# Loading q and k eight rows at a time in a channel-attention and GLU kernel

## The chip, the cores and the metric

One core of a Trainium2 chip. The metric is the device time of one execution in microseconds (us). Repeated executions of one kernel mostly agree within 0.3 us. The page of a profile is one profiled execution; its span is some 2 us shorter than the time. A line of a timeline gives start in us, duration in us, engine, line, operation, output<-inputs.

## The reference, cut to what matters

```python
# q, k, v: (4, 6016, 256) float32; tau = 1
qn = q / (norm(q, axis=1) + 1e-6)            # norms over the 6016 rows
kn = k / (norm(k, axis=1) + 1e-6)
a = softmax(kn.transpose(0, 2, 1) @ qn / tau)  # 256 x 256 per batch
x = (v @ a).reshape(24064, 256)
gate = sigmoid(x @ w_gate); val = x @ w_val    # 256 -> 1536
out = (gate * val) @ w_out                     # 1536 -> 256
```

## The kernel before

The rows of a batch lie 47 to a partition (6016 / 128). q, k and v are read from HBM as float32 and cast to bf16 by the DMA, four rows at a time: twelve groups a batch (in batch 0 thirteen, as the last group is split in two and one). For each group, PE adds eight matmuls of 256 columns to the scores s = q^T k, and VectorE (DVE) and ScalarE (ACT) square q and k for the norms.

Batch 0 is the head of the program: nothing can run beside it, since the weights of the later work, G = a^T w_gate / row sums and H likewise, need the whole batch. Batches 1 to 3 have their scores mixed into the GLU work of the batch before, at fixed places ("slots": one slot is one of the twelve 128-column parts of the hidden layer for one chunk of 512 rows). In the head, "fillers" keep PE working between groups: matmuls whose result nobody reads.

```python
def load_qk(b, t0, nt):                          # groups of four rows
    tiles = []
    for name, src in (("q", q), ("k", k)):
        tl = qkpool.tile([P, TPC, C], BF16, tag=name, name=name + "_sb")
        nc.gpsimd.dma_start(out=tl[:, :nt, :], in_=rows(src, b)[:, t0 : t0 + nt, :])
        tiles.append(tl)
    qk[b, t0] = tiles
...
for g, (t0, nt) in enumerate(groups0):           # the head
    engines = (nc.vector, nc.scalar) if g < last0 else (nc.scalar, nc.vector)
    sq = [squares(0, t0, nt, w, engines[w], acc[w] if g == 0 else None) for w in range(2)]
    if 0 < g < n_acc:                            # n_acc is 9
        for w in range(2):
            nc.vector.tensor_tensor(out=acc[w], in0=acc[w], in1=sq[w], op=ALU.add)
    for u in range(nt):
        score(0, t0, u)                          # 2 matmuls a row
    if g < n_acc:
        busy(5)                                  # five fillers
    elif g == n_acc:
        norm_mms(ps_n0, acc, TPC, True, False)
        norm_mms(ps_n0, sq, nt, False, False)
    elif nt == TPC:
        busy(2)
        norm_mms(ps_n0, sq, nt, False, False)
    ...                                          # groups 11 and 12
norms_sqrt(0); ...; norms_inv(0); ...            # 1 / norms, on ACT and DVE
spread_k(0, 0, pso, "o"); ...                    # ps_rk: needs 1 / norms
...
load_v(0, 1)                                     # POOL's DMAs, in this order
nc.gpsimd.dma_start(out=w_out_sb, in_=moe_w_out.rearrange("(t p) c -> p t c", p=P))
```

v is transposed by DMA (issued by SP), one transpose a chunk; only the first two chunks of batch 0 are transposed by PE.

Of the kernel before, what the change touches and what calls it, by code (L numbers as in the profile page):

```python
# [10 lines left out]
BF16 = mybir.dt.bfloat16  # L11
# [6 lines left out]
def kernel(  # L18
# [21 lines left out]
    P = nc.NUM_PARTITIONS  # L40
# [4 lines left out]
    B, N, C = q.shape  # L45
    CW, DFF = moe_w_gate.shape
    assert CW == C and C % P == 0 and N % P == 0 and DFF % P == 0
    NT = N // P
# [4 lines left out]
    TPC = 4  # L53
    CH = TPC * P
    NCH = (NT + TPC - 1) // TPC
    groups = [(t, min(TPC, NT - t)) for t in range(0, NT, TPC)]

    head = NT - NT % TPC
    groups0 = groups[: head // TPC] + [(t, n) for t, n in ((head, NT % TPC - 1), (NT - 1, 1)) if n > 0]

    def rows(x, b):
        return x[b].rearrange("(p t) c -> p t c", p=P)
# [3 lines left out]
    def pool(name, bufs, **kw):  # L66
        return ctx.enter_context(tc.tile_pool(name=name, bufs=bufs, **kw))

    consts = pool("consts", 1)
    qkpool = pool("qkpool", NCH)  # L70
    sqpool = pool("sqpool", 2)
    attp = pool("attp", 1)
    ghpool = pool("ghpool", 2)
# [13 lines left out]
    def mm(out, lhsT, rhs, start, stop, **kw):  # L87
        nc.tensor.matmul(out, lhsT=lhsT, rhs=rhs, start=start, stop=stop, **kw)  # L88


    qk = {}

    def load_qk(b, t0, nt):
        tiles = []
        for name, src in (("q", q), ("k", k)):
            tl = qkpool.tile([P, TPC, C], BF16, tag=name, name=name + "_sb")
            nc.gpsimd.dma_start(out=tl[:, :nt, :], in_=rows(src, b)[:, t0 : t0 + nt, :])  # L97
            tiles.append(tl)
        qk[b, t0] = tiles

    vs = {}

# [5 lines left out]


    t0, nt = groups0[0]  # L110
    qk[0, 0] = [qkpool.tile([P, TPC, C], BF16, tag=n, name=n + "_sb") for n in ("q", "k")]
    first_f32 = [consts.tile([P, nt, C], FP32, name=f"first{w}") for w in range(2)]
    for eng, tl, src in zip((nc.sync, nc.scalar), first_f32, (q, k)):
        eng.dma_start(out=tl, in_=rows(src, 0)[:, t0 : t0 + nt, :])
    nc.scalar.preload_act_table(ACT.Sqrt)
    load_qk(0, *groups0[1])

    ident_bf = consts.tile([P, P], BF16)
    make_identity(nc, ident_bf)
# [8 lines left out]

    nc.vector.tensor_copy(out=qk[0, 0][0], in_=first_f32[0])
    nc.scalar.copy(qk[0, 0][1], first_f32[1])  # L130
    for t0, nt in groups0[2:]:
        load_qk(0, t0, nt)
    load_v(0, 0)

# [18 lines left out]
    def score(b, t0, u):  # L153
        q_sb, k_sb = qk[b, t0]
        if t0 == 0 and u == 0:
            st.setdefault(b, {})["s"] = pss.tile([P, CB, C], FP32, tag="s", name="ps_s")
        ps_s = st[b]["s"]
        t = t0 + u
        for j in range(CB):
            mm(  # L160
                ps_s[:, j, :],
                q_sb[:, u, ds(j * P, P)],
                k_sb[:, u, :],
                start=(t == 0 and j == 0),
                stop=(t == NT - 1),
                skip_group_check=True,
            )

    def squares(b, t0, nt, which, engine, sq=None):
        src = qk[b, t0][which]  # L170
        if sq is None:
            sq = sqpool.tile([P, TPC, C], BF16, tag=f"sq{which}", name=f"sq{which}")
        if engine is nc.scalar:
            nc.scalar.activation(out=sq[:, :nt, :], in_=src[:, :nt, :], func=ACT.Square)  # L174
        else:
            engine.tensor_tensor(  # L176
                out=sq[:, :nt, :], in0=src[:, :nt, :], in1=src[:, :nt, :], op=ALU.mult
            )
        return sq

    def norm_mms(ps, sqs, nt, first, last, order=(0, 1)):

        for w in order:
            sq = sqs[w]
            for u in range(nt):
                for j in range(CB):
                    mm(
                        ps[:, w * CB + j : w * CB + j + 1],
                        sq[:, u, ds(j * P, P)],
                        ones_bf[:, 0:1],  # L190
                        start=(first and w == order[0] and u == 0 and j == 0),
                        stop=(last and u == nt - 1),
                        skip_group_check=True,
                    )
# [171 lines left out]
    def transpose_v(b, ci, ps=None, late=None):  # L366

        t0, nt = groups[ci]
        v_sb = vs.pop((b, ci))
        vT = vtpool.tile([P, TPC * CB, P], BF16, tag="vT", name="vT")  # L370
        flat = v_sb[:, :nt, :].rearrange("p t c -> p (t c)")
        if ps is None:
            nc.sync.dma_start_transpose(out=vT[:, : nt * CB, :], in_=flat)
        else:
            for n in range(nt * CB):
                nc.tensor.transpose(  # L376
                    out=ps[:, n, :], in_=flat[:, ds(n * P, P)], identity=ident_bf
                )
            half = nt * CB // 2
            nc.vector.tensor_copy(out=vT[:, :half, :], in_=ps[:, :half, :])  # L380
            (nc.scalar.copy if late is None else late)(vT[:, half : nt * CB, :], ps[:, half : nt * CB, :])
        vts[b, ci] = vT.rearrange("p (u cb) n -> p cb u n", cb=CB)
# [54 lines left out]
    def busy(n):  # L437

        ps = psg.tile([P, CH], FP32, tag="g", name="ps_busy")
        for _ in range(n):  # L440
            mm(ps, ones_bf, ones_wide, True, True)
# [8 lines left out]
    for g, (t0, nt) in enumerate(groups0):  # L450
        engines = (nc.vector, nc.scalar) if g < last0 else (nc.scalar, nc.vector)
        sq = [squares(0, t0, nt, w, engines[w], acc[w] if g == 0 else None) for w in range(2)]
        if 0 < g < n_acc:
            for w in range(2):
                nc.vector.tensor_tensor(out=acc[w], in0=acc[w], in1=sq[w], op=ALU.add)  # L455
        for u in range(nt):
            score(0, t0, u)
        if g < n_acc:
            busy(5)
        elif g == n_acc:  # L460
            norm_mms(ps_n0, acc, TPC, True, False)
            norm_mms(ps_n0, sq, nt, False, False)
# [3 lines that stand above are left out]
        elif g < last0:  # L466
            held = (sq, nt)
        else:
            norm_mms(ps_n0, *held, False, False)
            norm_mms(ps_n0, sq, nt, False, True, (1, 0))  # L470
# [28 lines left out]
    def side_work(b):  # L499


        side = {}

        def at(slot, fn, *a):
            side.setdefault(divmod(slot, FC), []).append((fn, a))

        for ci in range(NCH):
            nb, nci = (b, ci + 1) if ci + 1 < NCH else (b + 1, 0)
            lb, lci = (b, ci + 2) if ci + 2 < NCH else (b + 1, ci + 2 - NCH)
            if (nb, nci) == (0, 1):  # L510
                at(7, lambda: transpose_v(0, 1, psm.tile([P, TPC * CB, P], BF16, tag="m", name="ps_tp")))
            elif nb < B:
                at(ci * FC + 2, transpose_v, nb, nci)
            if lb < B:
                at(ci * FC + 0, load_v, lb, lci)
        n = b + 1
        if n == B:
            return side
        first, last = (14 if b == 0 else 0), 9 * FC
        for g, (t0, nt) in enumerate(groups):  # L520
            s0 = first + g * (last - first) // NCH
            at(max(0, s0 - 20), load_qk, n, t0, nt)
            for u in range(nt):
                at(first + (t0 + u) * (last - first) // NT, score, n, t0, u)
            if g == 0:
                at(s0, acc_start, n)
            for i, (fn, w) in enumerate(((acc_square, 0), (acc_add, 0), (acc_square, 1), (acc_add, 1))):
                at(s0 + 1 + 2 * i, fn, n, g, w)
        at(9 * FC + 9, norms_mm, n)
        for ci, s, *call in (  # L530
            (9, 0, wide_sqrt, n),
            (9, 2, wide_inv, n, 0),
            (9, 3, wide_inv, n, 1),
            (10, 0, wide_scale, n),
            (10, 0, exps, n, 0),
            (10, 0, exps, n, 1),
        ):
            side.setdefault((ci, FC + s), []).append((call[0], call[1:]))
        at(11 * FC + 0, sums_both, n)
        at(11 * FC + 0, gh_tiles, n)  # L540
        for i in range(len(gh_order)):
            at(11 * FC + min(i + 1, FC - 1), gh, n, i, *((pss, "s"), (psm, "m"))[i % 2])
        return side
# [61 lines left out]
```

## Time and profile before

| | before |
|---|---|
| time, median of 6 | 831.43 us (831.34 to 831.52) |
| PE busy | 817.8 of 829.6 us |
| granted PE clock | full, one core |
| packets on the loads' queue q0 | 23,920 |
| head: scores of group 10 begin | 31.73 us |
| head: norm matmuls end, ps_rk begins | 34.39, 35.30 us |

The prediction shows the lines on PE's waits, its timeline in the head and the traffic of the DMA queues. Three more matter later. They are from the timelines of PE, DVE and POOL (start in us, duration in us, engine, line, operation, output<-inputs), all of the kernel before, at the end of the head:

```profile
35.30 0.68 PE L88 MATMUL ps_rk<-ident_f,r 128*128 128x128 f32 x4
```

```profile
34.77 0.17 DVE L265 TENSOR_SCALAR r<-r 128x4 f32<-128x4 f32 x1
34.98 0.18 DVE L266 RECIPROCAL r<-r 128x4 f32<-128x4 f32 x1
```

### The profile page before, as it was taken

Reading aid. Unit: us, or ns where it says so; the run is one execution under the profiler, and the core shown is the slowest. Engines: PE = TensorE matmul, PEld = TensorE weight load, DVE = VectorE, ACT = ScalarE, POOL = GpSimd, SP = SyncE. Lnnn points to the kernel's source line nnn. Section 1 sums busy time; section 2 is a strip of 40 time slices with the busy share of each in tenths; the row PEclk is TensorE's granted clock in tenths of the full one; section 3 lists DMA queues with packets and bytes.
Section 4 is the critical chain, followed back from the end, with each engine's and each line's share of the span. In section 5 each row is a group of like instructions: output and inputs, shape, how many; then the busy total and the mean of one; then the engine's idle time right before and its main releaser. Section 6 shows DMA issues by size and latency. Waiting matters only on the chain.

```text
span 829.6 us, 13793 instructions
## 1 busy us (share of the span) xinstructions
PE 817.8 (99%) x5224; PEld 503.6 (61%) x5224; DVE 581.1 (70%) x998; ACT 391.9 (47%) x644; POOL 83.3 (10%) x159
## 2 busy tenths in 40 slices
PE   7899999999999999999999999999999999999998
PEld 4556666666666666665576666666566566666666
DVE  6577777777667777777767777777766666666664
ACT  4654444445644444444654444444655444444442
POOL 5531100002110100000210020000000000000000
PEclk9999999999999999999999999999999999999999
DMA  9999724326755553233874453233222323322211
GB/s 209 207 206 185 134 52 90 51 62 131 135 107 102 102 108 62 51 52 84 156 140 100 84 113 73 51 78 63 61 61 64 71 51 83 70 49 69 46 36 71
DMA packets 78739, 77.19 MB, mean 93 GB/s; under 512 B 50768, under 2 KB 55632, under 8 KB 78672
## 3 DMA queue, kind: packets, MB, share of 16 engines
q0 software_dynamic: 23920, 38.81, 28.3%
q1 hardware_dynamic: 54608, 36.97, 17.4%
q8 instruction: 41, 0.67, 0.3%
q10 hardware_dynamic: 144, 0.52, 0.2%
q14 instruction: 26, 0.21, 0.1%
HBM read 78.64 MB, written 24.64 MB: 125 GB/s over the span
## 4 chain that ended last, share of the span: by engine, by line
PE 95%; DMA 3%; POOL 0%; issue 0%; ACT 0%; DVE 0%; POOLq 0%; ACTq 0%
PE ps_o L88 30%; PE ps_val L88 29%; PE ps_gate L88 29%; PE ps_s L88 4%; DMA k_sb<-in_k_dram 3%; PE ps_gh L88 3%; PE ps_n L88 0%; PE ps_busy L88 0%; POOL q_sb L97 0%; ACT e_sb L294 0%; DVE hT L406 0%; ACT g_sb L405 0%; POOL k_sb L97 0%; PE ps_rk L88 0%; PE ps_tp L376 0%
## 5 line engine op out<-in xcount | busy, mean ns | idle before, releaser
L406 DVE TENSOR_TENSOR hT<-ps_val,g_sb 128x512 bf16<-128x512 f32 (+1 forms) x576 | 391.5, 680 | 214.6 <-ACT g_sb L405 209.3
L405 ACT ACTIVATE g_sb<-ps_gate 128x512 bf16<-128x512 f32 (+1 forms) x576 | 338.5, 589 | 386.0 <-PE ps_gate L88 378.4
L88 PE MATMUL ps_gate<-vT,gh_G 128*128 128x512 bf16 (+1 forms) x1152 | 337.7, 375 | 0.4 <-ACT g_sb L405 0.4
L88 PE MATMUL ps_val<-vT,gh_H 128*128 128x512 bf16 (+1 forms) x1152 | 337.5, 375 | 0.1
L88 PE MATMUL ps_o<-w_out_sb,hT 128*128 128x256 bf16 x2256 | 326.2, 273 | 0.0
L88 PEld LDWEIGHTS <-hT 128*128 128x128 bf16 x2256 | 220.8, 98 | 124.7
L88 PEld LDWEIGHTS <-gh_H 128*128 128x128 bf16 x1152 | 112.7, 98 | 131.0 <-issue 0.4
L88 PEld LDWEIGHTS <-gh_G 128*128 128x128 bf16 x1152 | 112.4, 98 | 38.0 <-issue 0.6
L106 POOL DMA_DIRECT2D v_sb<-in_v_dram x48 | 25.6, 534 | 623.6 <-DMA vT<-v_sb 501.3
L432 DVE COPY out_sb<-ps_o 128x256 f32<-128x256 f32 x188 | 77.9, 414 | 13.5 <-PE ps_o L88 13.5
L88 PE MATMUL ps_s<-k_sb,q_sb 128*128 128x256 bf16 x376 | 66.0, 272 | 5.6 <-DMA k_sb<-in_k_dram 4.3
L88 PEld LDWEIGHTS <-q_sb 128*128 128x128 bf16 x376 | 36.6, 98 | 14.7 <-issue 6.8
L215 DVE TENSOR_TENSOR acc<-acc,sq 128x1024 bf16<-128x1024 bf16 (+1 forms) x66 | 44.2, 670 | 0.0
L176 DVE TENSOR_TENSOR sq<-q_sb 128x1024 bf16<-128x1024 bf16 (+2 forms) x44 | 29.4, 668 | 2.7 <-DMA q_sb<-in_q_dram 2.7
L97 POOL DMA_DIRECT2D q_sb<-in_q_dram x48 | 26.4, 550 | 15.3 <-DMA q_sb<-in_q_dram 6.2
L97 POOL DMA_DIRECT2D k_sb<-in_k_dram x48 | 26.2, 545 | 13.9 <-DMA k_sb<-in_k_dram 8.6
L176 DVE TENSOR_TENSOR sq<-k_sb 128x1024 bf16<-128x1024 bf16 (+2 forms) x34 | 22.4, 658 | 0.9 <-ACT sq L174 0.9
L359 ACT ACTIVATE gh_G<-ps_gh,rrow 128x512 bf16<-128x512 f32 x21 | 14.4, 688 | 12.7 <-PE ps_gh L88 10.9
L88 PE MATMUL ps_busy<-ones_wide,ones_bf 128*128 128x512 bf16 x60 | 17.0, 416 | 1.6 <-DVE shift L127 1.6
L174 ACT ACTIVATE sq<-k_sb 128x1024 bf16<-128x1024 bf16 (+1 forms) x11 | 11.2, 1019 | 14.6 <-DMA k_sb<-in_k_dram 14.6
L361 DVE TENSOR_SCALAR gh_H<-ps_gh,rrow 128x512 bf16<-128x512 f32 x22 | 16.4, 744 | 1.6 <-PE ps_gh L88 1.6
L455 DVE TENSOR_TENSOR acc<-acc,sq 128x1024 bf16<-128x1024 bf16 x16 | 11.1, 692 | 5.6 <-ACT sq L174 5.4
(59 smaller groups left out, 117.7 us busy)
## 6 DMA issues: line engine op xcount, KB each, us to landing
out_dram<-out_sb SPq DMA_DIRECT2D x44, 512.0 KB, 2.9
v_sb<-in_v_dram POOLq DMA_DIRECT2D x44, 256.0 KB, 3.9
q_sb<-in_q_dram POOLq DMA_DIRECT2D x43, 256.0 KB, 7.0
k_sb<-in_k_dram POOLq DMA_DIRECT2D x43, 256.0 KB, 7.7
out_dram<-out_sb SPq DMA_DIRECT2D x4, 384.0 KB, 2.5
w_gate<-in_moe_w_gate_dram POOLq DMA_DIRECT2D x3, 256.0 KB, 6.8
w_val<-in_moe_w_val_dram POOLq DMA_DIRECT2D x3, 256.0 KB, 7.4
w_out_sb<-in_moe_w_out_dram POOLq DMA_DIRECT2D x1, 768.0 KB, 12.6
```

The source lines that it names most:

```text
L88: nc.tensor.matmul(out, lhsT=lhsT, rhs=rhs, start=start, stop=stop, **kw)
L97: nc.gpsimd.dma_start(out=tl[:, :nt, :], in_=rows(src, b)[:, t0 : t0 + nt, :])
L106: nc.gpsimd.dma_start(out=v_sb[:, :nt, :], in_=rows(v, b)[:, t0 : t0 + nt, :])
L174: nc.scalar.activation(out=sq[:, :nt, :], in_=src[:, :nt, :], func=ACT.Square)
L176: engine.tensor_tensor(out=sq[:, :nt, :], in0=src[:, :nt, :], in1=src[:, :nt, :], op=ALU.mult)
L215: nc.vector.tensor_tensor(out=acc[:, :nt, :], in0=acc[:, :nt, :], in1=st[b]["sq", w][:, :nt, :], op=ALU.add)
L359: nc.scalar.activation(out=dst, in_=ps, func=ACT.Copy, scale=r)
L361: nc.vector.tensor_scalar(out=dst, in0=ps, scalar1=r, scalar2=None, op0=ALU.mult)
L405: nc.scalar.activation(out=g_sb[:, :n], in_=ps_gate[:, :n], func=ACT.Sigmoid)
L406: nc.vector.tensor_tensor(out=hts[b, ci][:, f, :n], in0=ps_val[:, :n], in1=g_sb[:, :n], op=ALU.mult)
L432: nc.vector.tensor_copy(out=out_sb[:, s, :], in_=ps)
L455: nc.vector.tensor_tensor(out=acc[w], in0=acc[w], in1=sq[w], op=ALU.add)
```

## The change

The intent: larger DMA packets (8 KB read, 4 KB written) for q and k, to spend less on each packet while the head waits for DMA, and fewer instructions on POOL. Since the data now come two groups at a time, a sixth filler is to keep PE working in the longer gaps. Core of the diff:

```diff
-    qkpool = pool("qkpool", NCH)
+    qkpool = pool("qkpool", 8)
...
-            tl = qkpool.tile([P, TPC, C], BF16, tag=name, name=name + "_sb")
+            tl = qkpool.tile([P, 2 * TPC, C], BF16, tag=name, name=name + "_sb")
             nc.gpsimd.dma_start(out=tl[:, :nt, :], in_=rows(src, b)[:, t0 : t0 + nt, :])
             tiles.append(tl)
-        qk[b, t0] = tiles
+        for u in range(0, nt, TPC):
+            qk[b, t0 + u] = [tl[:, u : u + TPC, :] for tl in tiles]
...
-    load_qk(0, *groups0[1])
+    pairs = [(t, 2 * TPC) for t in range(TPC, head - 3 * TPC, 2 * TPC)]
+    loads0 = pairs + [(t, n) for t, n in groups0 if t >= pairs[-1][0] + 2 * TPC]
+    load_qk(0, *loads0[0])
...
         if g < n_acc:
-            busy(5)
+            busy(6)
...
-            at(max(0, s0 - 20), load_qk, n, t0, nt)
+            if g % 2 == 0:
+                at(max(0, s0 - 20), load_qk, n, t0, min(2 * TPC, NT - t0))
```

In batch 0 groups 1-2, 3-4, 5-6 and 7-8 become pairs; group 0 and groups 9 to 12 stay as they were.

More of the change, by code (lines that the diff above doesn't have):

```diff
@@ L110 @@
     t0, nt = groups0[0]
-    qk[0, 0] = [qkpool.tile([P, TPC, C], BF16, tag=n, name=n + "_sb") for n in ("q", "k")]
+    qk[0, 0] = [
+        qkpool.tile([P, 2 * TPC, C], BF16, tag=n, name=n + "_sb")[:, :TPC, :] for n in ("q", "k")
+    ]
     first_f32 = [consts.tile([P, nt, C], FP32, name=f"first{w}") for w in range(2)]
@@ L130 @@
     nc.scalar.copy(qk[0, 0][1], first_f32[1])
-    for t0, nt in groups0[2:]:
+    for t0, nt in loads0[1:]:
         load_qk(0, t0, nt)
```

## The prediction

> **What bounds the kernel now.** I read the page's totals first, then the waits of PE, then the chain of work that ended last, and last the DMA traffic in the stretches that these pointed to.
>
> ```profile
> PE 817.8 (99%) x5224; PEld 503.6 (61%) x5224; DVE 581.1 (70%) x998; ACT 391.9 (47%) x644; POOL 83.3 (10%) x159
> ```
>
> PE is busy 817.8 of 829.6 us. The table of stretches shows PE busy for all of 60 to 600 us and nearly all of the rest; idle time lies in the first 60 us, where some of the "busy" is filler besides (ps_busy). All waits of PE that the view of waits lists:
>
> ```profile
> PE ps_s L88 <- DMA k_sb<-in_k_dram: 4.3, 8, 1.4
> PE ps_busy L88 <- DVE shift L127: 1.6, 1, 1.6
> PE ps_s L88 <- ACT k_sb L130: 1.3, 1, 1.3
> PE ps_gate L88 <- ACT g_sb L405: 0.4, 1, 0.4
> PE ps_r L88 <- ACT e_sb L294: 0.2, 1, 0.2
> ```
>
> So the change can move the end only (a) in the head, where the scores of batch 0 wait for k, or (b) by creating a new wait. The timeline of PE in the head:
>
> ```profile
> 23.25 1.03 PE L88 MATMUL ps_s<-k_sb,q_sb 128*128 128x256 bf16 x8 [0.41 <-DMA k_sb<-in_k_dram]
> 24.12 1.24 PE L88 MATMUL ps_busy<-ones_wide,ones_bf 128*128 128x512 bf16 x5
> 26.72 1.03 PE L88 MATMUL ps_s<-k_sb,q_sb 128*128 128x256 bf16 x8 [1.36 <-DMA k_sb<-in_k_dram]
> 27.59 1.24 PE L88 MATMUL ps_busy<-ones_wide,ones_bf 128*128 128x512 bf16 x5
> 29.25 1.03 PE L88 MATMUL ps_s<-k_sb,q_sb 128*128 128x256 bf16 x8 [0.42 <-DMA k_sb<-in_k_dram]
> 30.12 0.54 PE L88 MATMUL ps_n<-ones_bf,acc 128*128 128x1 bf16 x16
> 30.53 0.54 PE L88 MATMUL ps_n<-ones_bf,sq 128*128 128x1 bf16 x16
> 31.73 1.03 PE L88 MATMUL ps_s<-k_sb,q_sb 128*128 128x256 bf16 x8 [0.67 <-DMA k_sb<-in_k_dram]
> 33.44 0.82 PE L88 MATMUL ps_s<-k_sb,q_sb 128*128 128x256 bf16 x6
> ```
>
> Groups come every 2.5 us, each when its k lands. One group takes 0.87 us of scores (start to start) and five fillers of 0.216. The 1.36 us gap is a transfer late by 1.0 us: there one 16 KB instruction fetch sits in the DMA engines (row "q8 instruction: 1" between 23.5 and 24.5 us, 6.1% of 16 us of engine time, so one engine for 0.98 us). The last wait for DMA in the head is the one that ends at 31.73; from there PE runs through scores and norms to 34.39.
>
> The DMA engines are full in the head. Three stretches with packets of different size, first q and k from 8 to 22 us (written packets of 2 KB), then w_out from 44 to 46 us (512 B):
>
> ```profile
> DMA packets 1607, 2.93 MB, mean 209 GB/s; under 512 B 176, under 2 KB 176, under 8 KB 1607
> ...
> DMA packets 778, 0.40 MB, mean 199 GB/s; under 512 B 0, under 2 KB 778, under 8 KB 778
> ```
>
> The GB/s count bf16 written; f32 is read at twice that, 418 GB/s.
>
> **What the Trainium skill says.** "DMA: Bandwidth & Descriptors", "Why small descriptors are slow (HBM only)", gives a fixed overhead of about 3 cycles a packet. The trace agrees that it is small: 512 B packets at 199 GB/s take 41.2 ns each over 16 engines, 2 KB ones at 209 take 156.8; a line through both is 2.7 ns + 38.5 ns per 512 B. "Perfetto Trace Analysis", "DMA Optimizations", says that batching from 2 KB to 4 or 8 KB can improve throughput dramatically; this trace doesn't promise that, as a packet a quarter the size costs only 5%. The DMA page's "Queues, rings and completion order", has each engine go round its queues packet by packet; the trace agrees: while a transpose (q1, 256 B packets) runs against the loads (q0),
>
> ```profile
> q0 software_dynamic: 193, 0.36, 94.1%
> q1 hardware_dynamic: 194, 0.05, 18.0%
> ```
>
> 193 packets stand against 194 in 2 us. "TensorE: Matmul & The Clock Gate", Part 1, gives some 3.4 us of idleness before the clock drops; no idle stretch of PE here is that long and the granted clock is 9 tenths or more in every slice.
>
> **The change, part by part.**
>
> *Packets.* For batch 0, eight loads of eight rows (q and k of groups 1-2, 3-4, 5-6, 7-8, which I call pairs) replace sixteen of four; the first and last groups stay as they are. Each such load saves every engine 8 packet overheads of some 3 ns and a semaphore write, about 0.03 us; eight loads: 0.22 us (an estimate). The last pair (groups 7, 8) lands 0.2 us before the group 8 of now.
>
> *Granularity.* A group can't start until its pair has landed. For the first three pairs this doesn't matter: with six fillers a group takes 0.87 + 6 x 0.216 = 2.17 us, a pair 4.34, and a pair lands every 4.95, so PE still waits for DMA (0.6 us per pair). But the last pair lands at T, and then PE has two groups to do before group 9, where now it has one. From T: group 7 0.87, fillers 1.30, group 8 0.87, fillers 1.30, group 9 0.87, its 32 norm matmuls 0.82: 6.03 us until group 10 may begin. Now group 10 begins 5.01 after group 8 (31.73 - 26.72), set by DMA. The head's end is thus bound by PE, not by DMA.
>
> *The fetch.* If T is 26.72 - 0.22 = 26.50, group 10 begins at 32.53 instead of 31.73: **0.8 us later**. But T holds the 1.0 us of the fetch. Fetches come as PE works through its instructions (41 of them for 10,448; mine to infer), the first with 222 started. Now these are in group 7 (26 per group); with 28 per group, group 7 begins at 214, and it then begins only at T. If the fetch therefore slips behind T, T is 25.5 and group 10 begins at 31.53: **0.2 us earlier**, which is also about when its k lands. I give this 55%. Average of the two: +0.25 us.
>
> *Fillers.* Nine more matmuls of 0.216 us. Seven lie in waits; the two after T are in the sum above. After the head PE never waits for the weights, which land no later than now.
>
> *Buffers and issue.* 8 buffers of 8 rows instead of 12 of 4. Batch 0 takes nine; the ninth reuses group 0's, free since 9 us. Batch 1 reuses pairs consumed by 33 us. No wait there. POOL issues 50 loads fewer, 0.54 us each, on an engine 10% busy: worth nothing.
>
> *The transpose of v chunk 2.* Its issue and landing:
>
> ```profile
> 49.15 1.34 SPq L373 DMA_TRANSPOSE vT<-v_sb  x1
> ...
> DMA to landing us min/median/max: 3.3/3.7/16.3
> ```
>
> The 16.3 is this one: 1,024 packets, 64 per engine, from about 53 to 65 us, each behind a 2 KB load packet (about 0.183 us a round, 0.026 above the 0.157 of a load packet alone). PE needs it for slot 24, which begins at 70.87: 5.4 us of slack. After the change POOL runs as far ahead as now, and the loads of batch 1 in that stretch are eight rows long. If a turn is one packet, a round with such a packet takes 2 x 0.157 - 0.003 + 0.026 = 0.337 us. In queue order the 64 rounds hold about 40 long packets and 24 of v: 40 x 0.337 + 24 x 0.183 = 17.9 us, from 53.0 to 70.9, plus 0.4 for landing and 0.6 if the stall near 63 us recurs: 71.3 to 71.9. Further, under load this transpose needs 4.1 us from issue to its first packet, against 2.0 for later ones; longer packets may add up to 2 us more. PE would want it at 70.7 (early head) or 71.7 (late head). So a **new wait of 0 to 3 us** on a transpose; with the chance that long packets take turns in smaller pieces, I count 0.8 us on average.
>
> Later batches: PE has no DMA wait, transposes run alone, k has over 3 us of slack at first use. Zero.
>
> Sum: 831.4 + 0.25 + 0.8 = 832.4, shaded to 832.3.
>
> **The rivals.**
>
> *The larger packets pay in full.* If per-packet cost were much larger than my line says, T would come 1 us or more earlier. For it: the head is DMA-bound and the chain of waits lists 3.3% for "DMA k_sb<-in_k_dram". Against it: 5% between 512 B and 2 KB, and even then PE needs 8.7 us after T. Time: about 830.5.
>
> *The head's tail goes to PE in full and nothing else.* For it: the sum of PE work after T. Time: 832.2.
>
> *The transpose stall comes in full.* For it: the 1:1 alternation. Against: a turn may be less than a packet, as nothing here shows packets over 4 KB read on q0. Time: 833 to 834.5.
>
> *All hidden.* The fetch slips, the transpose makes it: 831.2.
>
> **Range and chances.** Every mechanism is a few microseconds at most and 2% is 16.6 us. The runs before differ by 0.14 us, so the shift should be visible, but its sign is uncertain. 80%: 831.0 to 834.0. Within 2%: 0.98.
>
> **What would show it.** (1) q0's GB/s between 8 and 22 us: 211 to 212; over 215 and the packet cost was mis-sized. (2) The gap before each pair's scores: about 0.6 us or less, and no gap in front of groups 9 to 12. (3) The fetch's place, and whether the last pair begins at 25.5 or 26.5. (4) End of the head's norm matmuls at 34.2 or 35.2 against 34.39. (5) The first transpose's time to landing: over 20 us if a turn is a packet; near 16 if not. (6) A new PE wait on vT near 71 us. Wrong altogether if PE waits for k in batches 1 to 3, or if the clock drops in the head.

## More of the kernel before

```profile
34.78 0.56 POOL L106 DMA_DIRECT2D v_sb<-in_v_dram  x1
35.31 1.05 POOL L144 DMA_DIRECT2D w_out_sb<-in_moe_w_out_dram  x1
```

DVE forms 1 / norm (an addition of 0.17 us on 512 numbers, then the reciprocal) and is through at 35.16; POOL, at that time, writes the descriptors of v's and w_out's loads. PE's ps_rk needs r and starts right behind its fillers, without a wait.

## The result, and the profile after

The changed kernel takes 832.38 us (median of 6, 832.16 to 832.76) against 831.43 of before in the same rounds. The ratio is 1.0012, with a 95% interval from 0.9999 to 1.0025. The six executions of each do not overlap: it is slower by about 0.95 us. (Ratios here are the mean time of one kernel's runs over that of the other's of the same rounds, so not quite the ratio of the medians that are quoted.)

From the page of the changed kernel, the totals and the queue of the loads:

```profile
span 830.8 us, 13712 instructions
...
q0 software_dynamic: 17584, 38.80, 27.1%
```

The packets fell from 23,920 to 17,584 for the same bytes. PE's waits, all of them (waited for: us in total, times, longest):

```profile
PE ps_s L88 <- DMA k_sb<-in_k_dram: 3.8, 4, 1.5
PE ps_busy L88 <- DVE shift L133: 1.6, 1, 1.6
PE ps_s L88 <- ACT k_sb L136: 1.6, 1, 1.6
PE ps_rk L88 <- DVE r L272: 0.5, 1, 0.5
PE ps_gate L88 <- ACT g_sb L411: 0.4, 1, 0.4
PE ps_r L88 <- ACT e_sb L300: 0.2, 1, 0.2
```

There are four waits for k, one for each pair (1.49, 0.36, 0.48 and 1.44 us), instead of eight; no wait on vT; and one new wait, 0.5 us in front of ps_rk. The timeline of PE in the head, to be set beside the one in the prediction:

```profile
20.62 1.03 PE L88 MATMUL ps_s<-k_sb,q_sb 128*128 128x256 bf16 x8 [0.48 <-DMA k_sb<-in_k_dram]
...
26.56 1.03 PE L88 MATMUL ps_s<-k_sb,q_sb 128*128 128x256 bf16 x8 [1.44 <-DMA k_sb<-in_k_dram]
...
28.72 1.04 PE L88 MATMUL ps_s<-k_sb,q_sb 128*128 128x256 bf16 x8
...
30.89 1.04 PE L88 MATMUL ps_s<-k_sb,q_sb 128*128 128x256 bf16 x8
...
32.57 1.03 PE L88 MATMUL ps_s<-k_sb,q_sb 128*128 128x256 bf16 x8
...
34.92 0.44 PE L88 MATMUL ps_n<-ones_bf,sq 128*128 128x1 bf16 x12
...
36.55 0.68 PE L88 MATMUL ps_rk<-ident_f,r 128*128 128x128 f32 x4 [0.52 <-DVE r L272]
```

Left out are fillers (from 27.43, 29.59 and 35.23) and norm matmuls (from 31.76 and 32.17) among others. From the landing of the last pair at 26.56 PE has no gap until its norms are done. Group 10 begins 6.01 us later, at 32.57 instead of 31.73: 0.84 us lost. ACT had begun to square group 10's k at 31.61, so its data were there; PE was not. The second loss is between 34.92 and 36.55: ps_rk is 1.25 us later than before, of which 0.41 is new. DVE and POOL there:

```profile
35.61 0.59 DVE L271 TENSOR_SCALAR r<-r 128x4 f32<-128x4 f32 x1
36.23 0.18 DVE L272 RECIPROCAL r<-r 128x4 f32<-128x4 f32 x1
```

```profile
35.14 1.06 POOL L150 DMA_DIRECT2D w_out_sb<-in_moe_w_out_dram  x1
```

The small addition takes 0.59 us instead of 0.17 and ends at 36.20, just as POOL's issue of w_out does (35.14 + 1.06). POOL's issues hang on DMA and come when they did before (35.14 against 35.31); DVE's addition has moved 0.84 us later, into them.

From 36.55 on, everything is shifted: ps_rk by 1.25, the span by 1.2 (830.8 against 829.6). The profiled execution was the slowest of the six, so its 1.25 us is more than the 0.95 between the medians.

The transpose of v chunk 2 is as slow as feared and costs nothing. Its time to landing is the maximum in the view of SP's transposes, 16.3 before, now:

```profile
DMA to landing us min/median/max: 3.3/3.7/21.3
```

It is issued at 48.99, lands at 70.3, and PE begins the chunk that reads it near 72 us.

### The profile page after: what moved, and what is told of

Same layout as the page of the kernel before. It is cut to its first block, busy times and chain, and to the rows that moved or that the text cites. A ratio compares the mean times of both kernels' runs of the same rounds, so it can differ in the third digit from the quotient of the medians. Undisturbed runs are those within 1.5% of the kernel's fastest.

```text
span 830.8 us, 13712 instructions
## 1 busy us (share of the span) xinstructions
PE 818.2 (98%) x5219; PEld 504.5 (61%) x5233; DVE 581.1 (70%) x998; ACT 391.1 (47%) x644; POOL 59.9 (7%) x115
## 3 DMA queue, kind: packets, MB, share of 16 engines
q0 software_dynamic: 17584, 38.80, 27.1%
## 4 chain that ended last, share of the span: by engine, by line
PE 96%; DMA 2%; POOL 1%; DVE 0%; issue 0%; ACT 0%; POOLq 0%; ACTq 0%
PE ps_o L88 30%; PE ps_gate L88 29%; PE ps_val L88 29%; PE ps_s L88 4%; DMA k_sb<-in_k_dram 2%; PE ps_gh L88 2%; PE ps_n L88 0%; PE ps_busy L88 0%; POOL q_sb L98 0%; POOL k_sb L98 0%; ACT e_sb L300 0%; DVE hT L412 0%; ACT g_sb L411 0%; DVE r L271 0%; PE ps_rk L88 0%
## 5 line engine op out<-in xcount | busy, mean ns | idle before, releaser
L180 ACT ACTIVATE sq<-k_sb 128x1024 bf16<-128x1024 bf16 (+1 forms) x11 | 10.8, 1012 | 14.9 <-DMA k_sb<-in_k_dram 14.9
L98 POOL DMA_DIRECT2D q_sb<-in_q_dram x26 | 14.5, 559 | 15.9 <-DVE hT L412 5.5
L98 POOL DMA_DIRECT2D k_sb<-in_k_dram x26 | 14.1, 544 | 13.1 <-DMA k_sb<-in_k_dram 8.8
```

The costliest lines, as they stand in the source:

```text
L180: nc.scalar.activation(out=sq[:, :nt, :], in_=src[:, :nt, :], func=ACT.Square)
```

## The experiments

Twelve runs, five rounds each, each beside the kernel before: a, b, c, d, e, e2, f and g on one chip, a2, e3, h and j on the other. The two numbers that locate the loss are the starts of group 10 and of ps_rk in the profile; kernels with the head of before show 31.44 to 31.73 and 35.01 to 35.30.

| run | time, median us | before, same rounds | last pair starts | group 10 | ps_rk |
|---|---|---|---|---|---|
| changed kernel | 832.38 | 831.43 | 26.56 | 32.57 | 36.55 |
| a, no fillers behind last pair | 830.98 | 831.33 | (disturbed) | | |
| a2, the same again | 830.95 | 831.33 | 26.41 | 31.42 | 34.99 |
| b, five fillers everywhere | 831.71 | 831.30 | 26.39 | 31.96 | 35.54 |
| c, before with six fillers | 831.34 | 831.33 | no pairs | 31.56 | 35.13 |
| d, last pair split | 831.08 | 831.33 | groups 7, 8 apart | 31.31 | 34.88 |
| e, five fillers after groups 0-4 | 832.41 | 831.33 | 26.30 | 32.31 | 36.18 |
| e2, five after groups 0-6 | 832.41 | 831.30 | 26.40 | 32.41 | 36.27 |
| e3, three after groups 0-6 | 831.36 | 831.33 | 25.60 | 31.61 | 35.18 |
| f, pairs in the head only | 832.40 | 831.30 | 26.33 | 32.34 | 36.17 |
| g, pairs in later batches only | 831.62 | 831.30 | no pairs | 31.44 | 35.01 |
| h, w_out issued later | 832.01 | 831.33 | 26.29 | 32.30 | 35.87 |
| j, f without fillers behind last pair | 831.02 | 831.33 | 26.32 | 31.14 | 34.72 |

All intervals of the ratios are about 0.0013 to each side of the ratio and touch or include 1; the argument rests on groups of executions that lie apart, and on the profiles. Some runs hold an odd execution 1.2 to 1.8 us above their best (one each in e3, j, a2 and g), and the kernel before has smaller ones (831.80, 831.85, 831.91). In j, a2 and g the core's own span is longer and its mean granted clock is recorded as 0.998 (0.999 or 1.000 in their other executions); in e3 the span is 829.4, as in its others, so the extra microsecond lies outside it. None of them was profiled, and what they are stays open.

### f and g: which half of the change costs

```diff
 f: -            if g % 2 == 0:
    -                at(max(0, s0 - 20), load_qk, n, t0, min(2 * TPC, NT - t0))
    +            at(max(0, s0 - 20), load_qk, n, t0, nt)
 g: -    loads0 = pairs + [(t, n) for t, n in groups0 if ...]
    +    loads0 = groups0[1:]
    -            busy(6)
    +            busy(5)
 both: separate pools for the tiles of four and of eight rows
       (for the fours f has 12 buffers, as before; g has 8)
```

> The changed kernel's head (pairs, six fillers) with the later batches loaded by fours as before (own buffers for each). Theory (all of the loss is the head's tail): 832.3, and the first transpose of v takes about 16 us to landing as before. Rival (the long loads of batch 1 cost something, through the transpose or the order of v): 831.9 or less.

> The head of the kernel before (fours, five fillers) with the later batches loaded in eights. Theory: the first transpose takes 20 us or more to landing (a turn on a DMA engine is one packet, now twice as long), lands near 70.4 us, just before PE wants it at 70.9, and nothing is lost: 831.4, at most 0.2 more. Rival (the delayed transpose or later k costs PE): 832 or more and a PE wait on vT.

f takes 832.40 (832.35 to 832.43): the whole loss is in the head. Its slowest transpose takes 16.6 us. g takes 831.62 in the median, but 831.21 and 831.25 at best; its executions spread (831.90 and 832.98 too), more than g's expectation allowed, and its profiled execution (831.21) shows no wait on vT, though its slowest transpose takes 21.2 us. So the long loads of batch 1 do stretch the transpose by 5 us, and in the executions profiled that cost nothing, though by little: in g's profile it lands at 70.1 us and PE begins to read it at 70.57. Whether g's two slow executions were ones in which the transpose came too late can't be told without a profile of them; j, which has no long loads in batch 1, has one at 832.31 as well.

### a, a2 and d: the work behind the last pair

```diff
 a, a2:  -            busy(6)
         +            busy(6 if g < 7 else 0)
 d:      -    pairs = [(t, 2 * TPC) for t in range(TPC, head - 3 * TPC, 2 * TPC)]
         +    pairs = [(t, 2 * TPC) for t in range(TPC, head - 5 * TPC, 2 * TPC)]
```

> The changed kernel without the twelve fillers behind the last pair (groups 7 and 8). Theory (PE has too much to do after the last pair lands): the sum from the last pair to group 10 falls from 6.03 to 3.43 us, so group 10 waits for its own k again, at about 31.6 instead of 32.57 us; time 0.8 to 1.3 us below the changed kernel, about 831.3. Rival (the loss comes from the loads of batch 1 or the transpose, not from the head's tail): time stays at 832.4.

> The changed kernel, but groups 7 and 8 loaded apart, in runs of four rows (three pairs instead of four), fillers at six. Theory: group 8 alone is left when its k lands, so group 10 waits for its own k at 31.5 to 31.7; time about 831.3, a little below before thanks to six larger loads (0.16 us). Rival (large runs themselves slow the head or the later batches): 832.0 or more.

> The same kernel as the first of these runs, whose profiled execution ran with matmuls at half speed from its seventh microsecond on (1,756 us; the other four took 830.8 to 831.0). If that was the chip and not the kernel, all executions now take about 831.0, and the profile shows group 10 waiting for k at about 31.5 us. Rival: executions of 1,750 us again.

Four of a's executions took 830.84 to 831.02. The profiled one took 1,756 us: all its matmuls ran at about half speed, long before any filler that a removes. Every run begins at such a speed: its first fillers start 0.427 us apart, and 0.216 us apart once the clock is recorded as full (from 4.4 to 10.8 us on, by run). In a they start mostly 0.443 us apart, and no rise follows. Its record gives the granted clock as 1.0, but its trace holds no clock entry and its page no PEclk row, as all the others have, so that figure is no measurement. The row of the costliest PE group on its page, against 375 ns a matmul elsewhere:

```profile
L88 PE MATMUL ps_gate<-vT,gh_G 128*128 128x512 bf16 (+1 forms) x1152 | 649.9, 670 | 0.0
```

Five more executions of the same kernel in a2 showed nothing of the kind (830.90 to 831.20, one of 832.49), so it was that execution and not the kernel. It looks as if the speed of the start was never left; that is not shown, and the cause is open. In a2's profile PE waits for DMA again behind the last pair:

```profile
26.41 1.91 PE L88 MATMUL ps_s<-k_sb,q_sb 128*128 128x256 bf16 x16 [1.37 <-DMA k_sb<-in_k_dram]
28.95 1.03 PE L88 MATMUL ps_s<-k_sb,q_sb 128*128 128x256 bf16 x8 [0.64 <-DMA k_sb<-in_k_dram]
```

Groups 7 and 8 run together as sixteen matmuls, and group 9 now waits 0.64 us for its k; group 10 starts at 31.42 (without a wait for its own k, which a's and a2's expectations had; a wait of 0.25 us for DVE's squares comes just before it), and the time is 1.4 us below the changed kernel, 0.4 below before. d reaches the same by another way: with groups 7 and 8 loaded apart, fillers still six, it takes 831.08, and group 10 waits 0.21 us for its k at 31.31. Both show that large runs of rows do no harm in the head as long as the last of them doesn't leave PE behind.

### b and c: the fillers

```diff
 b:  changed kernel    -            busy(6)      c:  kernel before    -            busy(5)
                       +            busy(5)                           +            busy(6)
```

> The kernel before with six fillers instead of five. Theory: a group then takes 2.17 us of PE and its data come every 2.5 us, so the fillers lie in waits; 831.4 like before, within 0.15. Rival (the nine fillers cost their 9 x 0.216 = 1.9 us wherever they stand): 833.3.

> The changed kernel with five fillers everywhere, as before. PE's stream ahead of group 7 is then 200 instructions, as in the kernel before, where the first fetch (16 KB) began only once group 7 ran; ten fewer than the changed kernel's 214 weren't enough (the fetch came with 203 started). Theory: the fetch slips behind the last pair, which starts at about 25.4 us instead of 26.56; with 5.59 us of PE work behind it group 10 starts by 31.5, when its k lands; time about 831.2. Rival (the fetch comes at 24.4 us whatever PE does): last pair at 26.5, group 10 at 32.1, time about 831.9.

c takes 831.34, like before: nine fillers added where each group waits for DMA anyway cost nothing. b takes 831.71 (831.66 to 831.95): the theory of the fetch in b's expectation fell, and the rival's 831.9 is near. Two fillers fewer behind the last pair (one each after groups 7 and 8) shorten the way to group 10 from 6.01 to 5.57 us (31.96 - 26.39), a gain of 0.44. b's gain on the changed kernel is larger (832.38 - 831.71 = 0.67), since in b's profile the wait for DVE is gone too. The run e2 below differs from b in these two fillers alone and was timed in the same rounds: 832.41 against 831.71. Between their profiles group 10 moves by 0.45 us (32.41 to 31.96) and ps_rk by 0.73 (36.27 to 35.54), so 0.28 us lies with DVE.

### e, e2 and e3: the instruction fetch

The last pair starts 5.9 us behind the one before it, where DMA alone would bring it in 5.0. The prediction laid the difference to one fetch of 16 KB and gave 55% to its slipping behind the pair. In the changed kernel it stayed, as the traffic between 23.5 and 24.5 us shows (queue, packets, MB, share of 16 engines' time: 6.1% of 16 us is one engine for 0.98 us):

```profile
q0 software_dynamic: 50, 0.20, 98.4%
q8 instruction: 1, 0.02, 6.1%
```

These runs take instructions out of PE's stream ahead of group 7, by fillers, and leave the tail of six fillers.

```diff
 e:   -            busy(6)
      +            busy(6 if g > 4 else 5)
 e2:  +            busy(6 if g > 6 else 5)
 e3:  +            busy(6 if g > 6 else 3)
```

> The changed kernel with five fillers instead of six after groups 0 to 4, which takes ten instructions out of PE's stream ahead of the last pair and leaves everything after it. Theory: PE's first instruction fetch, which began with 209 instructions started (at 24.4 us), then falls behind the landing of the last pair; the pair lands about 1.0 us sooner (scores at 25.5 instead of 26.56), group 10 starts at 31.5; time about 831.4. Rival (the fetch is not PE's or not what delays the pair): last pair at 26.5, time 832.4 as the changed kernel.

> Five fillers after groups 0 to 6, six after groups 7 and 8: the tail of the changed kernel (6.03 us from the last pair to group 10) with a stream of 200 instructions ahead of group 7. Theory of the fetch: last pair at about 25.4, group 10 at 31.5, time about 831.2 although the tail is the long one. Rival: last pair at 26.5, group 10 at 32.5, time 832.3.

> Three fillers after groups 0 to 6, six after groups 7 and 8: 172 instructions ahead of group 7 instead of 214, the tail of the changed kernel untouched. With ten and fourteen fewer instructions the fetch stayed at 24.4 us, with 203 and 201 started. Theory: with 172 it can't have been reached before group 7 runs; the last pair starts at about 25.4, group 10 at about 31.4, time about 831.2. Rival (something else delays the pair by 1 us, the fetch stands beside it by chance): last pair at 26.4, group 10 at 32.4, time 832.4.

(The texts put the fetch at 24.4 us; the traces have its packet begin at 24.33 in the kernel before, at 24.18 in the changed one, at 24.1 to 24.2 in b, e and e2.) e and e2 missed: with ten and fourteen instructions fewer the fetch still came at 24.1 to 24.2 us and the time stayed at 832.41. With 42 fewer, e3, it left. In e3's profile the stretch from 23.5 to 27.5 holds no instruction packet; it is found from 29 to 30 us:

```profile
q0 software_dynamic: 130, 0.19, 105.2%
q8 instruction: 1, 0.02, 5.9%
```

and the last pair starts 0.80 us earlier than in e2, though the way from there to group 10 is the long one of 6.01 us:

```profile
25.60 1.03 PE L88 MATMUL ps_s<-k_sb,q_sb 128*128 128x256 bf16 x8 [1.72 <-DMA k_sb<-in_k_dram]
...
31.61 1.03 PE L88 MATMUL ps_s<-k_sb,q_sb 128*128 128x256 bf16 x8
```

The time falls by 1.05 us against e2, to 831.36. Of this, 0.80 us is the earlier pair (group 10 at 31.61 instead of 32.41); ps_rk comes 1.09 us earlier, as DVE's wait, the matter of run h, is gone too (the addition takes 0.17 us, not 0.46). One caution: e3 also has fourteen fillers fewer than e2 ahead of the pair, but those stood in waits (c), and the pair before it starts no earlier (20.68 against 20.45). So the fetch costs 0.8 us, and what follows from that, when it falls before the last pair of a head whose end PE sets. In the kernel before it made group 8 wait (1.36 us). In c it came earlier, at 21.8 us, and there the long wait (1.24 us) stands in front of group 7 instead: the wait goes where the fetch goes, and the time is the same.

### h: POOL's issue beside DVE

```diff
-    nc.gpsimd.dma_start(out=w_out_sb, ...)          # right behind load_v(0, 1)
+    ...                                             # behind load_v(0, 2), at slot 0 of batch 0
```

> The changed kernel with the load of w_out issued after that of v chunk 2, so that POOL's 1.06 us of descriptor work for it no longer stands where DVE computes 1/norm. Theory: DVE's small scalar operation on r (0.59 us in the changed kernel, ending together with POOL's issue; 0.17 before) goes back to 0.17 us, PE's wait in front of ps_rk is gone, and the time falls by 0.3 to 0.4 to about 832.0. Rival (the wait comes from elsewhere): wait stays, 832.4.

h takes 832.01 (831.86 to 832.35), 0.37 below the changed kernel, and the expectation holds. DVE's and POOL's lines in its profile:

```profile
35.34 0.17 DVE L270 TENSOR_SCALAR r<-r 128x4 f32<-128x4 f32 x1
```

```profile
35.81 1.03 POOL L505 DMA_DIRECT2D w_out_sb<-in_moe_w_out_dram  x1 [0.65 <-DMA w_gate<-in_moe_w_gate_dram]
```

The addition is back at 0.17 us, POOL writes w_out's descriptors after it, and ps_rk starts at 35.87, right behind PE's fillers and without a wait. e, e2 and f show the collision once more: the addition took 0.46 us from 35.35, 0.46 from 35.45 and 0.42 from 35.39, and POOL's issue of w_out ended at 35.83, 35.92 and 35.82. In b it began 0.18 us after POOL had begun with w_out and took 0.17 all the same, so not every overlap blocks; in the four that did, the changed kernel's included, DVE began 0.47 to 0.64 us into POOL's instruction.

### j: the best of both

```diff
 f plus:  -            busy(6)
          +            busy(6 if g < 7 else 0)
```

> Pairs in the head, six fillers but none behind the last pair, later batches by fours: group 10 waits for its own k at about 31.5 us, no transpose is slowed. Below both kernels: 830.9 to 831.1, with little spread. Rival (fillers or the order of batch 1 matter elsewhere): 831.3 or more.

j takes 831.02 (830.88 to 831.12, and one of 832.31), 0.3 us below before and level with a2 and d (830.95, 831.08). Its group 10 starts at 31.14, again without the wait for its own k that was expected; between groups 9 and 10 PE waits twice 0.25 us for DVE's squares and their sums, so DVE is what comes next there. These three are the best versions here; they beat the kernel before by 0.25 to 0.4 us, under 0.05%, which no interval separates from nothing.

## Why the prediction was right or wrong, point by point

The time was right almost to the digit (832.3 against 832.38), and partly by luck: in its sum of 1.05 us one term was 0.8 us too large (the transpose), and this made up for one that was 0.6 too small (tail and fetch together, +0.25 for 0.84) and one of 0.4 that it did not have (DVE).

- *PE's tail behind the last pair, 0.8 us.* Right. The sum said 6.03 us from the last pair to group 10, the profile says 6.01; 0.8 us later, the profile says 0.84. Removing the work (a2) or its lateness (d) removes the loss; f puts it in the head.
- *The fetch slips behind the last pair, 55%.* Wrong. It stayed, at 24.2 us, ahead of the pair, which started at 26.56 where 26.50 was given for that case. The step failed in counting instructions as started on PE: the fetch came with 209 started here, 222 in the kernel before, and 201 to 203 in b, e and e2, so the count at which it begins is not a fixed number of started instructions. That a slip would bring the pair about 1 us sooner was nearly right (e3 against e2: 0.80). The term of the sum was +0.25, as an average of two cases; the case that came was +0.8.
- *A wait for the transpose, 0.8 us on average.* Wrong. The mechanism was right: the transpose's packets take turns with the loads' one for one, with 8 KB packets too, as the changed kernel's traffic between 54 and 56 us shows,

```profile
q0 software_dynamic: 112, 0.40, 98.0%
q1 hardware_dynamic: 111, 0.03, 10.1%
```

  and its landing went from 16.3 to 21.3 us. But the estimate had it land at 71.3 to 71.9 with up to 2 us more; it landed at 70.3. Its first packet came 3.9 us after the issue, as in the kernel before (the prediction had read 4.1 there), and not up to 2 us later; from there to the landing it took 17.4 us where the sum had 18.3 to 18.9; and the late head moved PE's need by another 1.2 us. No profile shows a wait on vT, so the term is zero; with the head of before the margin was about 0.4 us (g, a2).
- *What the sum did not have.* DVE's addition held up while POOL writes w_out's descriptors, 0.42 us in the profiled execution and 0.37 between the medians of the changed kernel and h. It follows from the first term: what is late by 0.84 us meets work that isn't. The prediction listed what POOL's issues cost POOL (nothing) and not what they do to DVE.
- *Larger packets save 0.22 us.* Too small to matter, and its size is not settled: the last pair started 0.16 us before group 8 of the kernel before, with the fetch in both, but that start differs by 0.27 us between the profiles that share this head (26.29 in h to 26.56). The stretch from 8 to 22 us shows 214 GB/s where 211 to 212 was forecast, but at its edges 16 packets of 4 KB are 2% of its 2.99 MB; the step from one pair's scores to the next (15.64 to 20.62, 4.98 us, against 15.71 to 20.72 before, 5.01) says 0.6%.
- *Nothing in later batches, nothing from POOL's fewer instructions, fillers free in waits.* Right (no new wait behind the head; f; c), though POOL's loads fell by 44 and not by 50 (q and k together, 96 to 52 on the pages). And the gap before a pair, forecast at about 0.6 us, was 1.49 us for the first one, which has to land whole before PE can begin; with DMA setting the pace behind it, that cost nothing.

Of the rivals, "the head's tail goes to PE in full and nothing else" (832.2) was nearest.

## What to carry to other kernels

When transfers are made larger, ask what is left to do after the last one lands, not only how fast they flow: the coarser grain puts two groups of work behind the last landing, and filler work that was free in waits is paid for there. Keep the last transfers small or the work behind them bare. And when a chain moves by a fraction of a microsecond against another engine's schedule, look at which operations now stand side by side.

## What the Trainium skill lacked or had wrong

- "SBUF — State Buffer", "Who interferes with whom": the page has DVE and GpSimd share a port pair, names tensor_scalar among the operations that may take it, and says that whichever comes second blocks fully. The runs agree: DVE's addition took 0.42 to 0.59 us instead of 0.17 and ended with POOL's issue of w_out, and moving that issue (h) removed it; that the ports are the reason is the page's word, not the runs'. Its rule covers both orders, but its worked warning is of a DVE operation that starves a GpSimd DMA; it lacks the other one, that the issue of one DMA held a DVE addition up by some 0.4 us on the critical path. And it has the pair taken for the whole instruction, where in run b an addition that began 0.18 us into POOL's instruction of 1.06 us was not delayed (spans on POOL are rough).
- "Perfetto Trace Analysis", "DMA Optimizations": the page says that batching from 2 KB to 4 or 8 KB can improve throughput dramatically. It speaks of the size of transfers, and the prediction set it beside packets. Here packets went from 4 to 8 KB read and loads from 256 to 512 KB written, and the gain was 0.6% (4.98 against 5.01 us a pair); where the gain ends the page doesn't say.
- No page that I read draws the consequence of taking turns by packet when packets differ in size: the transpose of 256 B packets went from 16.3 to 21.3 us to landing when the loads beside it doubled their packets.
- "Runtime: NRT & Kernel Launch", "Instruction fetch mechanics": the page has the fetch in blocks of 16 KiB by a DMA queue of its own and calls its cost mostly hidden. It lacks what it can cost a load beside it: one such packet held one DMA engine for about 0.98 us, and the last pair started 0.80 us later in e2, whose fetch fell before it, than in e3, whose fetch came after.
- "TensorE: Matmul & The Clock Gate", Part 1: the page has a half-rate clock as the state in which PE begins. It lacks a busy execution that stays at such a speed to its end, as one of run a seems to have done (1,756 us; 670 ns a matmul against 375).
